# Locality-hashed attention with a gated projection: a planner that reckons with one queue of transfers, sigmoids by table, and a small load on another queue

## The chip, the cores and the metric

The kernel runs on one core of one Trainium2 chip. The metric is device time in microseconds of one execution. The core's engines run side by side, each through its own instructions in their order: TensorE (PE) multiplies matrices, VectorE (DVE) and ScalarE (ACT) work element by element and read its results, GpSimd (POOL) works element by element in on-chip memory, and SyncE (SP) issues transfers. Semaphores let an instruction of one engine wait for another engine or for a transfer.

## The reference

Attention over 4 batches, 8 heads, 768 rows and 64 columns per head, where a row sees only the rows with the same six hash bits; then a gated projection of the 3072 x 512 result, with 1536 hidden columns. Cut to what matters:

```python
q_bits = (np.einsum('bhsd,dk->bhsk', q, proj) > 0)           # six bits -> bucket; the same for k
mask = q_bucket[:, :, :, None] == k_bucket[:, :, None, :]
scores = np.where(mask, scale * np.matmul(q, k.transpose(0, 1, 3, 2)), -1e9)
attn = np.exp(scores - np.max(scores, axis=-1, keepdims=True))
attn = attn / (np.sum(attn, axis=-1, keepdims=True) + 1e-09)
x = np.matmul(attn, v)                                        # -> (3072, 512)
gate = 1.0 / (1.0 + np.exp(-(x @ w_gate)))
out = gate * (x @ w_val) @ w_out
```

The weights arrive as 64-bit floats and are turned into 32-bit ones on the chip.

## The kernel before, in words

**Stages.** The attention takes two heads at a time: 16 pairs, each in two groups of three 128-row tiles, 32 groups in all. For a pair, q and k are loaded (`load`, L968 and L977), turned on TensorE (`turn`, L1034), rounded to high and low parts (`high` L1054, `low` L1057), hashed (`hash_`, L1069; for the first pair `hash_first`, L1015) and the bits made (`bits`, L1076) and spread by small transfers (L1080, L1087). For a group come scores (L1162 for the bits, L1168 for the products), the row minimum that also evacuates them (`maximum`, VectorE, L1178), the exponential (`exponent`, ScalarE, L1186), turning of the exponentials (`turned`, L1219), a copy out of the banks (`whole`, L1226, on ScalarE or VectorE), the product with v (`values`, L1236), a reciprocal of the sums (`inverse`, L1193 on) that goes through memory (`told` L1200, `spread` L1207), the division on GpSimd (`divided`, L1246) and a store (L1249).

**The gated projection** has 12 blocks of hidden columns. Two of them (`J1 = 2`) are worked off during the attention, one unit for each batch and half of its rows, eight units: `moe_early` makes two gate products and two value products (`product`, L531), passes the gates through a sigmoid, multiplies (`gated`, L547 to L552), and makes an output product (L568). The other blocks follow after the attention, in `moe_pair` (L758, L877), fully on TensorE. Meanwhile the weights are converted (`converted`, L348 to L382) and split into parts (`split`, L405 to L415), which are stored and fetched again.

**The sigmoid in `moe_early`.** The batches 0 to 2 (six units) share the time with the attention. There ScalarE makes `exp(-z)` (L590), and VectorE adds one, bounds it and takes the reciprocal (`inverted`, L559 and L560). Batch 3 comes after the last attention group and uses ScalarE's sigmoid directly (`direct`).

**The order.** Each piece of work is a `Task` with a priority, an engine (or a choice of engines), a duration in ns, the tasks it waits for, and tokens for buffers that it takes and gives. `Plan.order` plays all tasks through with these durations, once, when the kernel is built: at each moment every free engine takes the ready task with the lowest key whose tokens are there. The sequence that comes out is the order in which each engine's instructions are written. On the chip nothing is reordered: a task that comes later than planned holds up what stands behind it on its engine. TensorE's tasks are also charged for a change of its tile division (`LEAVE`, `BEGIN`), and it may wait a while for another task of the same division (`PATIENCE`).

A transfer is a task of `sp`: 600 ns of issue, and a `tail` until it has landed, 2000 ns plus a ns for 200 bytes, whatever else is under way; where transfers crowd, a larger number of bytes is written instead (`CROWDED`). At most eight are reckoned to be under way (`landings`).

**The start.** The hash projection, 64 x 6 numbers, is loaded twice into a tile of weights by ScalarE's queue (`load_projection`, L277) behind the first q; `hash_weights` (L282 to L288, VectorE) then lays out the weights of the first hash. GpSimd clears tiles first (up to L294).

Of the kernel before, what the change touches and what calls it, by code (L numbers as in the profile page):

```python
# [24 lines left out]
HUGE = 2.0**126  # L25
# [4 lines left out]
SEEN = {"pe": 260, "act": 140, "pool": 130, "dve": 130, "sp": 0}  # L30
# [11 lines left out]
IN_FLIGHT = 8  # L42


class Task:
# [7 lines left out]
    def __init__(self, key, options, after, take, give, tail, kind, begun):  # L53
        self.key, self.options, self.take, self.give, self.tail = key, options, take, give, tail
# [12 lines left out]
class Plan:  # L67
# [5 lines left out]
    def __init__(self, stock):  # L73
        self.stock, self.tasks = dict(stock), []
        self.landings = [0] * IN_FLIGHT

    def add(self, key, engine, ns=None, emit=None, after=(), take=(), give=(), tail=0, kind="all", begun=()):
        options = engine if isinstance(engine, list) else [(engine, ns, emit)]
        t = Task((key, len(self.tasks)), options, after, take, give, tail, kind, begun)
        self.tasks.append(t)  # L80
        return t

    def order(self):
# [24 lines left out]
        while events:  # L108
# [10 lines left out]
            while again:  # L119
                again = False  # L120
                for e in SEEN:
# [58 lines left out]
def lsh_attention_glu_kernel(ctx, tc, q, k, v, proj, w_gate, w_val, w_out, out):  # L180
    nc = tc.nc
# [92 lines left out]
    def load_projection():  # L274
        for half in range(2):
            at_ = half * HS + NB
            nc.scalar.dma_start(hw["w"][half * D : (half + 1) * D, at_ : at_ + NB], proj)  # L277
# [57 lines left out]
    def converted(key, n, j, late, which, after, first):  # L335
# [48 lines left out]
        a = dma(key, CROWDED if late else 524288, load, after=after + last_load[late], take=[raw_])  # L384
# [4 lines left out]
        c1 = add(key, "dve", 440, mantissa, after=[b1], **both)  # L389
        c2 = add(key, "dve", 700, whole, after=[c1], **both)  # L390
        d = add(key, "dve", 700, signed, after=[b2, c2], take=["port"], give=[raw_, "port"])
        return z, add(key, "pool", 1300, lambda: scaled(nc.gpsimd), after=[d], **both)

    def split(key, src, to, size, late, after, give, tile_of=None):
# [16 lines left out]
        h = add(key, "act", 60 + 500 * part_, high, after=after, take=[wk] if tile_of is None else [])  # L411
        low_ = add(key, "pool", 100 + 1200 * part_, low, after=[h], take=["port"], give=give + ["port"])
        if tile_of is not None:
            return low_, low_
        return low_, dma(key, CROWDED if late else 1024 * size, lambda: nc.sync.dma_start(to, f(z["w"])), after=[low_], give=[wk])  # L415
# [19 lines left out]
    def combined(key, n, js, late, after):  # L435
# [26 lines left out]
        on = lambda fn: [("pool", 750, lambda: fn(nc.gpsimd)), ("dve", 350, lambda: fn(nc.vector))]  # L462
# [24 lines left out]
    def load_x(u, b, g, stored, ending):  # L487
# [19 lines left out]
        a = add(FIRST, "sp", 1200, load, after=stored + in_turn["x"], take=["xr"], tail=2000 + 786432 // 200)  # L507
# [50 lines left out]
    def inverted(j):  # L558
        nc.vector.tensor_scalar(sig[:, j], sig[:, j], 1.0, HUGE, op0=ALU.add, op1=ALU.min)  # L559
        nc.vector.reciprocal(sig[:, j], sig[:, j])  # L560

# [12 lines left out]
    def moe_early(key, b, g, stored, pace):  # L574
# [9 lines left out]
        for j in range(J1):  # L584
# [3 lines left out]
                FIRST, "act", 490,  # L588
                lambda j=j, z=z, fn=AF.Sigmoid if direct else AF.Exp, by=1.0 if direct else -1.0:
                    nc.scalar.activation(sig[:, j], z["acc"][:, :GN], fn, scale=by),  # L590
# [5 lines left out]
        else:  # L596
            s_ = [add(FIRST, "dve", 800, lambda j=j: inverted(j), after=[zs[j]], take=["port"], give=["port"]) for j in range(J1)]
# [40 lines left out]
    def x_pair(u, b, last_use):  # L638
# [35 lines left out]
        on = lambda fn: [("dve", 960, lambda: fn(nc.vector))]  # L674
        z["ready"], got = {}, {}

        def raw(name):
            got[name] = dma(
                FIRST + 0.5, 1200000 if u == "0_0" else 393216, lambda: load(name), after=stored[b, int(name[1]) - 1] + [later["switch"]], take=[f"r{name}"],
# [8 lines left out]
        def pieces_of(name):  # L688
            h = add(FIRST, "act", 850, lambda: high(name), after=[got[name]], take=[f"x{name}"])
# [28 lines left out]
    def fetch_piece(at_, js, slot, n, m, after, first):  # L718

        def go():  # L720
# [11 lines left out]
            1e3, CROWDED if first else CROWDED // 4, go,  # L732
# [8 lines left out]
    def group(key, at_, n, js, slot, x, sig_, final, free_w, hslot, prev):  # L741
# [34 lines left out]
        def snap(m, name):  # L776
            told[name] = add(
                FIRST, "act", 480, lambda: nc.scalar.copy(tile_(name, "sn"), bank[m]), after=[done[m]], take=["sn"], give=["z"],  # L778
            )

        def plus(m, y, name, after=(), give=("z",), tag=None):
            def go():
# [3 lines left out]
                FIRST, "dve", 560, go, after=[done[m], told[y]] + list(after), take=[tag] if tag else [], give=list(give),  # L786
            )

        def finish(where):
            a = told[where]  # L790
            if n == "g":
                sig_[where] = z, add(
                    FIRST, "act", 490, lambda: nc.scalar.activation(z[where], z[where], AF.Sigmoid), after=[a]
# [20 lines left out]
            c = add(FIRST, "act", 510, hi, after=[b], take=[f"h{hslot}{jj}{uu}"])  # L814
# [34 lines left out]
    def moe_pair(key, i, b, prev):  # L849
# [45 lines left out]
        def ended(t, prev, first, last):  # L895
# [15 lines left out]
            if first:  # L911
# [4 lines left out]
                FIRST, "dve", 690, lambda: nc.vector.tensor_add(obs[t], accs[t], obs[t]), after=[prev, ended_[t]],  # L916
# [37 lines left out]
    def pair(i):  # L954
# [134 lines left out]
        if i == 0:  # L1089
            pass  # L1090
        here = {
            n: add(t0 - 10.72, "act" if i == 0 and n == "q" else "sp", 1200 if n == "q" else 2400,
                   lambda n=n: load(n, nc.scalar if i == 0 and n == "q" else nc.sync), tail=4000, take=[n + "r"],
# [3 lines left out]
        if i == 0:  # L1097
            first_loads.extend(here.values())
            hw["loaded"] = add(t0 - 10.5, "act", 1200, load_projection, after=[])
            hw["landed"] = add(0, "pool", 0, lambda: None, after=[hw["loaded"], add(0, "pool", 4500, lambda: None)])  # L1100
# [25 lines left out]
        else:  # L1126
            a = add(t0 - 2.6, "pe", 4 * MM, hash_, after=plains + [hw["task"]], take=["two"], kind="hash")
            bits_ = add(t0 - 2.6, "dve", 480, bits, after=[a], give=["two"])
            needs.append(add(t0 - 2.6, "sp", 1200, spread_q, after=[bits_], tail=2500))
            needs.append(add(t0 - 2.6, "sp", 2400, lambda: spread_k(nc.sync), after=[bits_], tail=2500))  # L1130
        for m, n in enumerate("qk"):
            n_ = t0 - 3.4 + m * 0.5
            b_ = add(n_, [("act", 690, lambda n=n: high(n, nc.scalar.copy)), ("dve", 870, lambda n=n: high(n, nc.vector.tensor_copy))],
                     after=[plains["kq".index(n)]])
            ways = [("dve", 960, lambda n=n: low(n, nc.vector)), ("pool", 2000, lambda n=n: low(n, nc.gpsimd))]
# [5 lines left out]
            if n == "q" and i:  # L1141
                needs += [add(n_, "sp", 1200, lambda x=x: swapped(x), after=[y], tail=4000) for x, y in (("h", b_), ("l", c_))]
        if i == 0:
            first_loads.extend(needs)
        v_here = dma(t0 - 5, 393216, load_v, take=["vr"], after=first_loads[:2] + [last_loads.get("v")])
# [5 lines left out]
    def attend(i, g, z, needs, v_here):  # L1151
# [100 lines left out]
        for t in range(GT):  # L1252
# [16 lines left out]
        a = add(n, "dve", 560, inverse, after=exps, take=["sv"], give=["su"])  # L1269
        a = add(n, "sp", 600, told, after=[a], tail=2500, give=["sv"])  # L1270
# [122 lines left out]
```

## Time and profile before

| | |
|---|---|
| median of 3 runs | 1007.04 us (1006.73 to 1011.49) |
| the profiled execution | 1011.25 us, of which the span of the instructions is 1009.5 us |
| TensorE busy | 976.2 us (97%) |
| VectorE busy | 793.6 us (79%) |
| ScalarE busy | 544.8 us (54%) |
| GpSimd busy | 270.4 us (27%) |
| mean granted TensorE clock | 0.991 |
| first scores (L1162) | 18.78 us after the first instruction |

The numbers come from one profiled execution. A busy share is a mean over stages with different limits. Matrix products are pipelined, so a busy TensorE need not be at its peak, and a lowered clock shows as busy time. The "chain that ended last" is followed back from the last instruction, at each step to what released it or to the instruction ahead of it on its engine; "issue" in it is time in which the engine waited for nothing that the profile shows.

### The profile page before, as it was taken

To read this page: it belongs to the slowest core of one execution; us is meant where nothing else is said; L and a number is where in the kernel's file an instruction comes from. 1 tells how busy PE (TensorE), PEld (TensorE's weight loads), DVE (VectorE), ACT (ScalarE), POOL (GpSimd) and SP (SyncE) were. 2 spreads that over 40 slices of the span, in tenths; PEclk is the share of its full clock that TensorE was granted. 3 is DMA by queue.
4 is the path that set the end of the run, shared out by engine and by line. 5 is a ranking of instruction groups with operands and counts; after the bars stand their busy time and mean duration, and the time that the engine had idled before them with its cause. 6 is when DMAs were issued, how large, how long until landed. Compare 5 with 4: busy or idle time off the path is not lost.

```text
span 1009.5 us, 20877 instructions
## 1 busy us (share of the span) xinstructions
PE 976.2 (97%) x8091; PEld 781.9 (77%) x8092; DVE 793.6 (79%) x1467; ACT 544.8 (54%) x1016; POOL 270.4 (27%) x243
## 2 busy tenths in 40 slices
PE   7999997999999989899999999999999999999998
PEld 4666565666666666666679999999989989999897
DVE  6888997788798877788848877788777778787864
ACT  3878874777867857677634442353333425242330
POOL 1234463635555546355430121211100000000000
PEclk9999998999999999999999999999999999999999
DMA  5555584656676557455469977569469680505121
GB/s 132 130 161 166 136 226 143 191 171 192 204 221 179 186 166 221 150 163 184 143 221 397 370 242 283 203 239 357 153 201 368 212 281 10 188 17 172 35 91 62
DMA packets 144346, 190.95 MB, mean 189 GB/s; under 512 B 64728, under 2 KB 103032, under 8 KB 144248
## 3 DMA queue, kind: packets, MB, share of 16 engines
q1 hardware_dynamic: 142520, 189.24, 57.9%
q8 instruction: 63, 1.03, 0.4%
q10 hardware_dynamic: 1728, 0.40, 0.2%
q14 instruction: 35, 0.29, 0.1%
HBM read 127.41 MB, written 49.28 MB: 175 GB/s over the span
## 4 chain that ended last, share of the span: by engine, by line
PE 80%; DVE 12%; DMA 2%; ACT 2%; issue 2%; SPq 1%; POOL 0%; DVEq 0%; POOLq 0%; ACTq 0%
PE yo L877 16%; PE pv L1236 10%; PE sc L1168 6%; PE tp L1219 5%; DVE e L1178 5%; PE zo L568 4%; PE sc L1162 3%; PE zv L531 2%; PE zg L531 2%; PE z1g L758 2%; PE z4v L758 2%; PE z1v L758 2%; PE z6g L758 2%; PE z5g L758 2%; PE z2g L758 2%
## 5 line engine op out<-in xcount | busy, mean ns | idle before, releaser
L1186 ACT ACTIVATE e<-e,st 128x768 f32<-128x768 f32 x192 | 179.0, 933 | 64.2 <-DVE e L1178 64.1
L1178 DVE TENSOR_SCALAR_CACHE_REDUCE e<-sc 128x768 f32<-128x768 f32 x192 | 176.3, 950 | 33.9 <-PE sc L1168 33.2
L1236 PE MATMUL pv<-ef,vr 128*64 128x384 f32 x768 | 140.6, 499 | 2.6 <-ACT ef L1226 2.5
L1219 PEld LDWEIGHTS tp<-ident,e 64*128 64x128 f32 x2304 | 86.1, 139 | 47.3 <-issue 16.4
L1219 PE MATMUL tp<-ident,e 64*128 64x64 f32 x2304 | 98.5, 227 | 11.1 <-DVE e L1178 6.8
L1226 ACT COPY ef<-tp 128x768 f32<-128x768 f32 x107 | 84.0, 795 | 22.0 <-PE tp L1219 21.4
L1226 DVE COPY ef<-tp 128x768 f32<-128x768 f32 x85 | 80.7, 952 | 17.4 <-PE tp L1219 17.0
L1236 PEld LDWEIGHTS pv<-ef,vr 128*64 128x64 f32 x768 | 49.0, 137 | 57.0 <-issue 46.2
L1168 PE MATMUL sc<-kh,ql 64*128 64x384 f32 x192 | 90.5, 472 | 0.0
L1168 PE MATMUL sc<-kh,qsl 64*128 64x384 f32 x192 | 90.5, 471 | 0.0
L1162 PE MATMUL sc<-kb,qb 64*128 64x384 bf16 x384 | 65.6, 332 | 7.9 <-DVE e L1178 4.4
L1168 PE MATMUL sc<-kh,qh 64*128 64x384 f32 x192 | 64.7, 337 | 0.0
L1168 PE MATMUL sc<-kh,qsh 64*128 64x384 f32 x192 | 64.7, 337 | 0.0
L1168 PE MATMUL sc<-kl,qsh 64*128 64x384 f32 x192 | 64.4, 336 | 0.0
L1168 PE MATMUL sc<-kl,qh 64*128 64x384 f32 x192 | 64.4, 335 | 0.0
L1162 PEld LDWEIGHTS <-qb 64*128 64x128 bf16 x384 | 22.2, 94 | 51.7 <-issue 43.0
L778 ACT COPY snm1g<-z1g 128x384 f32<-128x384 f32 x20 | 9.6, 479 | 79.8 <-PE z1g L758 79.7
L916 DVE TENSOR_TENSOR ol<-yo,ol 128x512 f32<-128x512 f32 x36 | 24.8, 688 | 29.4 <-PE yo L877 29.4
L382 POOL TENSOR_TENSOR exg<-mfg,exg 128x512 f32<-128x512 f32 x12 | 15.7, 1305 | 109.5 <-DVE exg L377 109.5
L877 PE MATMUL yo<-wo,gh 128*128 128x512 f32 x144 | 44.5, 390 | 0.0
L1057 POOL TENSOR_TENSOR kl<-kx,kh 128x768 fp32r<-128x768 f32 x16 | 29.9, 1870 | 38.7 <-DVE kh L1054 26.2
L1246 POOL TENSOR_TENSOR xs<-xs,rb 128x384 f32<-128x384 f32 x32 | 33.2, 1039 | 24.7 <-DVE xs L1243 15.7
(590 smaller groups left out, 2851.8 us busy)
## 6 DMA issues: line engine op xcount, KB each, us to landing
wg<-kg SPq DMA_DIRECT2D x33, 512.0 KB
wv<-kv SPq DMA_DIRECT2D x33, 512.0 KB
ra<-xd SPq DMA_DIRECT2D x32, 384.0 KB
wo<-ko SPq DMA_DIRECT2D x22, 512.0 KB
part<-ob SPq DMA_DIRECT2D x36, 256.0 KB
kg<-pkg SPq DMA_DIRECT2D x15, 512.0 KB
kv<-pkv SPq DMA_DIRECT2D x15, 512.0 KB
kr<-in_k_dram SPq DMA_DIRECT2D x64, 96.0 KB
```

The lines of the kernel that those rows point to most:

```text
L531: nc.tensor.matmul(z["acc"][:, :GN], a[:, wc], x[xx][c // 2][:, c % 2, :], start=(c == 0 and i == 0), stop=(c == KC - 1 and i == 2),)
L568: nc.tensor.matmul(acc, a[:, slot, ts_], w, start=(first and i == 0), stop=(last and i == 2))
L758: nc.tensor.matmul(bank[m], a[:, wc], x[xx, block][:, c, :], start=(c == 0 and i == 0), stop=(c == 1 and i == 2),)
L877: nc.tensor.matmul(accs[t], a[:, ts_], w, start=(start and jj == 0 and q == 0), stop=(stop and jj == 1 and q == 2),)
L1162: nc.tensor.matmul(sc[:, j, :GN], z["qb"][rows, beyond if j else c], z["kb"][rows, h], start=True, stop=False, tile_position=(j * D, 0),)
L1168: nc.tensor.matmul(sc[:, j, :GN], q_[rows, c], z["k" + x][rows, h * GN : (h + 1) * GN], start=False, stop=(m == 2), tile_position=(j * D, 0),)
L1178: nc.vector.tensor_scalar(sp(e), gz["sc", t, h][:, :, :GN], MASKED, None, op0=ALU.min, op1=ALU.min, accum_out=gz["st", t][:, h : h + 1],)
L1186: nc.scalar.activation(e, e, AF.Exp, bias=st[:, h : h + 1], scale=-1.0, accum_out=gz["su"][:, h * GT + t : h * GT + t + 1],)
L1219: nc.tensor.transpose(tp[:, r, at_ : at_ + D], gz["e", t, h][rows, c * P : (c + 1) * P], ident[rows, rows], tile_position=(r * D, 0),)
L1226: copy(gz["ef", c].rearrange("p (n r d) -> p r n d", r=2, d=D), gz["tp", c][:, :, :GN].rearrange("p r (n d) -> p r n d", d=D),)
L1236: nc.tensor.matmul(gz["pv"][rows, :GN], z["v"][:, h, c], gz["ef", c][:, h * GN : (h + 1) * GN], start=(c == 0), stop=(c == NC - 1), tile_p ...
L1246: nc.gpsimd.tensor_mul(gz["xs"], gz["xs"], gz["rb"])
```

## The change

- Sigmoid: for batches 0 to 2, ScalarE copies both gate products out of their banks, then runs one sigmoid over both at once (768 columns). `inverted` and its two VectorE instructions go.
- Transfers in the plan: a transfer moves its data in one queue shared by all (`moving`), for a time given with the task, mostly bytes / 355 ns; it begins at the earliest 900 ns after the issue begins and is seen 1000 ns after its data. `CROWDED` goes.
- Periods in the plan: nearly all durations on VectorE, ScalarE, GpSimd and SP are set anew.
- The projection: `load_projection` issues from GpSimd's queue and is a task of `pool`. The time at which its landing is reckoned moves from a task of `pool` (4500 ns) to an engine of the plan only (`timer`, 4000 ns).

```diff
+BEFORE, BEHIND_IT = 900, 1000
...
-                    if e == "sp" and t.tail:
-                        free[e] = max(now, self.landings[0]) + ns
-                        self.landings = self.landings[1:] + [free[e] + t.tail]
+                    landed = 0
+                    if t.dmas:
+                        n_, moved = t.dmas
+                        if e == "sp":
+                            free[e] = max(now, self.landings[0]) + ns
+                        self.moving = max(self.moving, free[e] - ns + BEFORE) + moved
+                        landed = max(self.moving, free[e] + BEFORE // 2) + BEHIND_IT - free[e]
+                        if e == "sp":
+                            self.landings = (self.landings + [free[e] + landed] * n_)[n_:]
                     at(free[e], "free", e)
-                    seen = free[e] + t.tail + SEEN[e]
+                    seen = free[e] + (landed or SEEN[e])
...
-            nc.scalar.dma_start(hw["w"][half * D : (half + 1) * D, at_ : at_ + NB], proj)
+            nc.gpsimd.dma_start(hw["w"][half * D : (half + 1) * D, at_ : at_ + NB], proj)
...
-    CROWDED = 1600000
-
     def dma(key, nbytes, emit, **kw):
-        return add(key, "sp", 600, emit, tail=2000 + nbytes // 200, **kw)
+        return add(key, "sp", 550, emit, dmas=(1, nbytes / 355), **kw)
...
-        b1 = add(key, "dve", 440, exponent, after=[a], take=[token] * first + ["port"], give=["port"])
-        b2 = add(key, "act", 700, shifted, after=[b1])
+        b1 = add(key, "dve", 345, exponent, after=[a], take=[token] * first + ["port"], give=["port"])
+        b2 = add(key, "act", 620, shifted, after=[b1])
...
-    def inverted(j):
-        nc.vector.tensor_scalar(sig[:, j], sig[:, j], 1.0, HUGE, op0=ALU.add, op1=ALU.min)
-        nc.vector.reciprocal(sig[:, j], sig[:, j])
...
-                FIRST, "act", 490,
-                lambda j=j, z=z, fn=AF.Sigmoid if direct else AF.Exp, by=1.0 if direct else -1.0:
-                    nc.scalar.activation(sig[:, j], z["acc"][:, :GN], fn, scale=by),
+                FIRST, "act", 490 if direct else 375,
+                lambda j=j, z=z, fn=AF.Sigmoid if direct else AF.Copy: nc.scalar.activation(sig[:, j], z["acc"][:, :GN], fn),
...
-            s_ = [add(FIRST, "dve", 800, lambda j=j: inverted(j), after=[zs[j]], take=["port"], give=["port"]) for j in range(J1)]
+            s_ = [add(FIRST, "act", 3400, lambda: nc.scalar.activation(sig, sig, AF.Sigmoid), after=zs)] * J1
...
-        a = add(FIRST, "sp", 1200, load, after=stored + in_turn["x"], take=["xr"], tail=2000 + 786432 // 200)
+        a = add(FIRST, "sp", 1050, load, after=stored + in_turn["x"], take=["xr"], dmas=(2, 2600))
...
-            hw["loaded"] = add(t0 - 10.5, "act", 1200, load_projection, after=[])
-            hw["landed"] = add(0, "pool", 0, lambda: None, after=[hw["loaded"], add(0, "pool", 4500, lambda: None)])
+            hw["loaded"] = add(t0 - 10.5, "pool", 1200, load_projection)
+            hw["landed"] = add(0, "timer", 0, lambda: None, after=[hw["loaded"], add(0, "timer", 4000, lambda: None)])
...
-            b_ = add(n_, [("act", 690, lambda n=n: high(n, nc.scalar.copy)), ("dve", 870, lambda n=n: high(n, nc.vector.tensor_copy))],
+            b_ = add(n_, [("act", 735, lambda n=n: high(n, nc.scalar.copy)), ("dve", 480, lambda n=n: high(n, nc.vector.tensor_copy))],
...
-                    n + 1.25, "act", 1025, lambda t=t, h=h: exponent(t, h), after=[least[h]] + exps[-1:],
+                    n + 1.25, "act", 928, lambda t=t, h=h: exponent(t, h), after=[least[h]] + exps[-1:],
...
-        a = add(n, "sp", 600, told, after=[a], tail=2500, give=["sv"])
-        spread_ = add(n, "sp", 1200, spread, after=[a], tail=3500, take=["rb"])
+        a = add(n, "sp", 680, told, after=[a], dmas=(1, 80), give=["sv"])
+        spread_ = add(n, "sp", 1250, spread, after=[a], dmas=(2, 680), take=["rb"])
```

More of the change, by code (lines that the diff above doesn't have):

```diff
@@ L74, in __init__, with add @@
         self.stock, self.tasks = dict(stock), []
-        self.landings = [0] * IN_FLIGHT
-    def add(self, key, engine, ns=None, emit=None, after=(), take=(), give=(), tail=0, kind="all", begun=()):
+        self.landings, self.moving = [0] * IN_FLIGHT, 0
+    def add(self, key, engine, ns=None, emit=None, after=(), take=(), give=(), dmas=None, kind="all", begun=()):
         options = engine if isinstance(engine, list) else [(engine, ns, emit)]
-        t = Task((key, len(self.tasks)), options, after, take, give, tail, kind, begun)
+        t = Task((key, len(self.tasks)), options, after, take, give, dmas, kind, begun)
         self.tasks.append(t)
@@ L382, in scaled @@
             eng.tensor_mul(f(z["ex"]), f(z["mf"]), f(z["ex"]))
-        a = dma(key, CROWDED if late else 524288, load, after=after + last_load[late], take=[raw_])
+        a = dma(key, 600000, load, after=after + last_load[late], take=[raw_])
         last_load[late] = [a]
         both = dict(take=["port"], give=["port"])
-        b1 = add(key, "dve", 440, exponent, after=[a], take=[token] * first + ["port"], give=["port"])
-        b2 = add(key, "act", 700, shifted, after=[b1])
[L389 to L392, printed above, removed]
+        b1 = add(key, "dve", 345, exponent, after=[a], take=[token] * first + ["port"], give=["port"])
+        b2 = add(key, "act", 620, shifted, after=[b1])
+        c1 = add(key, "dve", 345, mantissa, after=[b1], **both)
+        c2 = add(key, "dve", 605, whole, after=[c1], **both)
+        d = add(key, "dve", 605, signed, after=[b2, c2], take=["port"], give=[raw_, "port"])
+        return z, add(key, "pool", 1250, lambda: scaled(nc.gpsimd), after=[d], **both)
     def split(key, src, to, size, late, after, give, tile_of=None):
@@ L678, in raw @@
             got[name] = dma(
-                FIRST + 0.5, 1200000 if u == "0_0" else 393216, lambda: load(name), after=stored[b, int(name[1]) - 1] + [later["switch"]], take=[f"r{name}"],
+                FIRST + 0.5, 440000, lambda: load(name), after=stored[b, int(name[1]) - 1] + [later["switch"]], take=[f"r{name}"],
             )
@@ L731, in fetch_piece @@
         made[at_, js, n, m] = last_fetch[role] = dma(
-            1e3, CROWDED if first else CROWDED // 4, go,
+            1e3, 1024 * (HF if m == 3 and n != "o" else DM), go,
             after=[made_piece[key_], later["switch" if slot else "first"], last_fetch.get(role)] + after, take=[role],
@@ L777, in snap @@
             told[name] = add(
-                FIRST, "act", 480, lambda: nc.scalar.copy(tile_(name, "sn"), bank[m]), after=[done[m]], take=["sn"], give=["z"],
+                FIRST, "act", 385, lambda: nc.scalar.copy(tile_(name, "sn"), bank[m]), after=[done[m]], take=["sn"], give=["z"],
             )
@@ L785, in plus @@
             told[name] = add(
-                FIRST, "dve", 560, go, after=[done[m], told[y]] + list(after), take=[tag] if tag else [], give=list(give),
+                FIRST, "dve", 476, go, after=[done[m], told[y]] + list(after), take=[tag] if tag else [], give=list(give),
             )
@@ L792, in finish @@
                 sig_[where] = z, add(
-                    FIRST, "act", 490, lambda: nc.scalar.activation(z[where], z[where], AF.Sigmoid), after=[a]
+                    FIRST, "act", 430, lambda: nc.scalar.activation(z[where], z[where], AF.Sigmoid), after=[a]
                 )
@@ L813, in finish @@
             low_ = lambda eng: eng.tensor_sub(z["h", where][1], z[where], f(z["h", where][0]))
-            c = add(FIRST, "act", 510, hi, after=[b], take=[f"h{hslot}{jj}{uu}"])
+            c = add(FIRST, "act", 425, hi, after=[b], take=[f"h{hslot}{jj}{uu}"])
             sig_["h", where] = add(
@@ L1288, in attend @@
         a = add(n - 6, either(summed), after=[prev], take=["xs"], give=["one"] + ["moe"] * ends)
-        a = add(n - 4, "pool", 1050, divided, after=[a, spread_], take=["port"], give=["rb", "port"])
+        a = add(n - 4, "pool", 965, divided, after=[a, spread_], take=["port"], give=["rb", "port"])
         stored[b, g].append(dma(n, 196608, store, after=[a], give=["xs"]))
```

39 lines of the change are left out of this document (19 added, 20 removed).

## The prediction

> **What bounds the kernel now.** I read the page's busy shares and chain first, then stretches of the span cut where TensorE stops, then the chain in order of time, then the start. The page:
>
> ```profile
> PE 976.2 (97%) x8091; PEld 781.9 (77%) x8092; DVE 793.6 (79%) x1467; ACT 544.8 (54%) x1016; POOL 270.4 (27%) x243
> PE 80%; DVE 12%; DMA 2%; ACT 2%; issue 2%; SPq 1%; POOL 0%; DVEq 0%; POOLq 0%; ACTq 0%
> ```
>
> TensorE is the bound, but 12% of the chain that ended last, 121 us, is VectorE. The stretches tell where; columns are the stretch, its length, each engine's busy time, granted clock, DMA share, GB/s:
>
> ```profile
> 0.00:18.78 18.78, 13.54 (x75) 6.66 (x77) 10.20 (x40) 5.47 (x7) 4.51 (x13) 0.91 0.75 168
> 18.78:160.00 141.22, 131.86 (x1664) 86.28 (x1665) 118.20 (x238) 112.12 (x208) 59.56 (x47) 1.00 0.61 164
> 160.00:180.00 20.00, 17.08 (x141) 12.71 (x138) 16.05 (x26) 8.82 (x17) 7.67 (x8) 0.83 0.36 118
> 180.00:285.00 105.00, 104.61 (x1210) 71.26 (x1211) 88.58 (x171) 80.86 (x153) 55.06 (x47) 1.00 0.64 194
> 285.00:292.00 7.00, 5.86 (x76) 4.59 (x74) 6.94 (x9) 3.76 (x9) 1.27 (x1) 1.00 0.47 134
> 292.00:360.00 68.00, 67.07 (x759) 45.88 (x756) 54.02 (x104) 50.84 (x97) 40.46 (x37) 1.00 0.63 191
> 360.00:378.00 18.00, 14.53 (x154) 10.10 (x154) 15.88 (x26) 10.68 (x20) 5.52 (x5) 0.91 0.45 142
> 416.00:430.00 14.00, 11.31 (x120) 9.79 (x120) 11.15 (x21) 9.34 (x19) 4.09 (x3) 0.88 0.18 66
> 430.00:495.00 65.00, 64.25 (x754) 41.77 (x750) 55.84 (x114) 49.62 (x95) 35.11 (x33) 1.00 0.56 177
> 495.00:520.00 25.00, 22.45 (x218) 15.14 (x217) 16.34 (x24) 13.91 (x25) 10.30 (x9) 1.00 0.38 131
> 544.00:1009.50 465.50, 461.62 (x2421) 430.01 (x2419) 355.13 (x623) 163.60 (x309) 25.83 (x24) 1.00 0.56 198
> ```
>
> From 544 us on TensorE is busy but for the last 3.9 us; nothing the change touches can shorten that. Before, the loss sits in five short stretches. Idle time plus time lost to a lowered clock (length times one minus the clock): 160 to 180: 2.9 + 3.4 = 6.3; 285 to 292: 1.1; 360 to 378: 3.5 + 1.6 = 5.1; 416 to 430: 2.7 + 1.7 = 4.4; 495 to 520: 2.6. Together **19.5 us**. The rest of the attention stage is idle for 9.4 us up to 160 and 0.4 + 0.9 + 0.8 after it, **11.5 us**. Now the chain in order of time (start, length, what):
>
> ```profile
> 161.88 2.55 DVE sig L560
> 165.30 1.85 issue
> 221.84 2.55 DVE sig L560
> 286.62 2.55 DVE sig L560
> 362.00 2.55 DVE sig L560
> 365.82 2.33 issue
> 406.64 2.44 issue
> 495.93 2.55 DVE sig L560
> 508.08 2.43 issue
> ```
>
> Each of the five stretches has a reciprocal of the gate (L560) in it or ahead of it. The four "issue" pieces are reciprocals too: each lies behind one and lasts about as long. So nine of the twelve stand on the path, and five of these groups leave TensorE without work. The prices behind it:
>
> ```profile
> L559 DVE TENSOR_SCALAR sig<-sig x12: 296/355/1156, 161.5 to 507.7; 128x384 f32<-128x384 f32 x12
> L560 DVE RECIPROCAL sig<-sig x12: 2552/2553/2554, 161.9 to 508.0; 128x384 f32<-128x384 f32 x12
> L590 ACT ACTIVATE sig<-zg x16: 468/490/493, 142.7 to 540.3; 128x384 f32<-128x384 f32 x16
> L590 ACT ACT_TABLE_LOAD  x1: 1283/1283/1283, 519.7 to 519.7; - x1
> L778 ACT COPY snm1g<-z1g 128x384 f32<-128x384 f32 x20 | 9.6, 479 | 79.8 <-PE z1g L758 79.7
> L1226 ACT COPY ef<-tp 128x768 f32<-128x768 f32 x107 | 84.0, 795 | 22.0 <-PE tp L1219 21.4
> ```
>
> The old plan charged 800 ns for a task (tensor_scalar, reciprocal) that lasts 355 + 2553 = 2908 ns. Two per unit put VectorE 4.2 us behind its plan, and everything behind them in its queue was late: the maxima (L1178) that free score banks and release ScalarE's exponentials.
>
> **The change, part by part.**
>
> *Sigmoid.* VectorE loses 12 x 2.908 = 34.9 us of its 793.6. ScalarE gets, per unit, one sigmoid over 768 elements and two table loads, since exponentials stand on both sides. The sigmoid is the 384-element one plus what 384 more cost in a copy: 490 + (795 - 479) = 806 ns. A unit is 806 + 2 x 1283 = 3.37 us, six units 20.2 us; the last may need no load back. The new plan charges 3.4 us, so it knows the block. The twelve exponentials become copies: 12 x (490 - 479) = 0.1 us. What hides the block: in the five stretches ScalarE is idle for 11.2, 3.2, 7.3, 4.7 and 11.1 us. What now waits: exponentials queued behind it, and both gate products (L547), which wait for both gates where the first could go after its own; the value products (L531) lie between and cover that. What the block still costs TensorE no row shows. From below it is 0, for it fits the idle time just counted; from above it is 5.1 us per unit, the stretch 360 to 378 over again. I take 1.1 us, the smallest stall of the five, as the block is no longer than that idle time in four of the five and in the plan: 6 x 1.1 = 6.6. So this part: -19.5 + 6.6 = **-12.9 us**.
>
> *The projection through GpSimd's queue.* The start:
>
> ```profile
> 0.73 1.28 ACT L235 ACT_TABLE_LOAD   x1 [0.73 <-PEq L1377]
> 2.02 0.20 ACT L235 ACTIVATE warm<-warm 128x1 f32<-128x1 f32 x1
> 2.93 4.18 ACTq L277 DMA_DIRECT2D hw<-in_proj_dram  x2
> 3.06 0.24 POOL L294 MEMSET su<- 128x32 f32 x3
> 6.99 0.17 DVE L282 TENSOR_SCALAR hw<-hw 64x6 f32<-64x6 f32 x1 [2.37 <-DMA hw<-in_proj_dram]
> 9.10 1.80 POOL L1057 TENSOR_TENSOR kl<-kx,kh 128x768 fp32r<-128x768 f32 x1 [5.79 <-ACT kh L1054]
> 9.44 1.49 DVE L282 TENSOR_SCALAR hw<-hw 64x6 f32<-64x6 f32 x1 [2.29 <-DMA hw<-in_proj_dram]
> 11.57 2.90 PE L1015 MATMUL hk<-kx,w 128*128 128x384 f32 x4 [3.45 <-DVE w L288]
> 14.26 1.56 PE L1015 MATMUL hq<-qx,w 128*128 128x384 f32 x4
> 18.78 0.34 PE L1162 MATMUL sc<-kb,qb 64*128 64x384 bf16 x2
> ```
>
> Two issues leave ScalarE's queue, which has nothing due until the first transposes come, and go to GpSimd's, behind its memsets (end 3.30) and ahead of its first subtraction at 9.10, which sat idle 5.79 us before. No engine's work moves; what can move is the second landing at 9.42, on which the hash weights wait. On ScalarE's queue the two were issued over 4.18 us, behind two loads of q. On GpSimd's own queue there is nothing ahead. If they take no longer than the first did (issued 2.93, seen at 6.99, 4.06 us), the second lands near 3.3 + 0.6 + 4.06 = 8.0: 1.4 us earlier. Then VectorE's second step also comes before GpSimd's subtraction, beside which it took 1.49 us against 0.17 alone (1.3 us), and the first hash, which stood idle 3.45 us before and ran in a start with a mean clock of 0.91, may take the second's 1.56 instead of 2.90 us (1.3 us). Upper bound: 4.0 us. Lower bound: an issue on GpSimd that takes the whole 4.18 us again lands at 3.3 + 4.18 + 2.9 = 10.4, a loss of 1.0. I take **-3.0 us**, nearer the end where the two follow-on gains come with an arrival before 9.1. On this the Trainium skill ("SBUF — State Buffer", section "SBUF: two separate sides") speaks against the change: a DMA issued from GpSimd has its descriptors written by GpSimd, which a VectorE operation in a two-port mode locks out meanwhile. No run here shows it; by it the term would be 0 and the sum -10.9 us.
>
> *One queue of transfers, measured periods.* No instruction's work changes, only who comes when in each queue. Two transfers of the chain:
>
> ```profile
> 153.38 3.92 DMA kg<-pkg
> 411.46 3.08 DMA rd<-sv
> ```
>
> A 512 KB store took 3.92 us from issue on; the old plan said 0.6 + 2.0 + 2.6 = 5.2, the new one 0.9 + 1.5 + 1.0 = 3.4 with nothing ahead of it and more with a backlog. The small store of the sums took 3.08; the old plan said 0.6 + 2.5 = 3.1, the new one says 0.7 + 0.45 + 1.0 = 2.1 at least, so here it reckons too early; its reader is GpSimd's division, off TensorE's path. The engines' periods come down to the rows: 1025 to 928 for an exponential (933 on the page), 700 to 605, 870 to 480 for a cast. What a new order is worth no row gives: at best the 11.5 us of idle time that I have not tied to the gates, at worst two new stalls like the first stretch, 12.6 us. I take +2: the transfers' reckoning is nearer for the large ones, too early for the small.
>
> **Sum:** -12.9 - 3.0 + 2 = -13.9 us. The profiled execution took 1011.25 us (span 1009.5), which gives 997.3; it stands 4.2 us over the median of 1007.04, and from that the forecast is 1007.0 - 13.9 = **993**.
>
> **Rivals.**
> *The block on ScalarE takes most of it back.* For: exponentials must wait 3.4 us at a time. Against: ScalarE's idle time above. At 2.6 us each the six cost 15.6, and the start brings 2: 1007 - 19.5 + 15.6 - 2 = 1001, and with the order's +2 about 1003.
> *ScalarE becomes the late engine (slower).* If exponentials come late by so much that TensorE stops and its clock falls each time, each of the six units costs the 5.1 us of 360 to 378: 30.6, less 19.5 and less 3, plus the order's 2: 1017. It decides once the block outlasts ScalarE's idle time in a stretch, as in 285 to 292, where it has 3.2 us for 3.4.
> *Loads cost more than their row.* If ScalarE also stood still after each load by as much again as the load, a unit would be 3.37 + 2 x 1.28 = 5.9 us, 15 us more in all, and with all of it on the path the time 993 + 15 = 1008. Against: the first load ends at 2.01 and the next activation starts at 2.02. Such a rule stands in the Trainium skill ("ScalarE: Activation LUTs", section "What ACT_TABLE_LOAD costs"): 1283 ns and some 1380 ns of drain. The 1283 agrees with this trace, the drain after the load it does not show.
> *More than I count.* The new order also takes the 11.5 us and the block costs nothing: 1007 - 19.5 - 11.5 - 3 = 973; half of the former, 979.
> *The projection is not earlier:* 996; inside the forecast's range.
>
> **How the numbers follow.** About 0.5%, 5 us, is what a measurement of this kernel can tell (its three runs span 4.8). Forecast 0.60 (own range 985 to 1001), more than I count 0.08: faster 0.68. The block takes it back 0.14, loads dearer 0.04: within 0.5% 0.18. Slower 0.14. The range reaches from 980, half of the "more" case, to 1010, which leaves out the slower case and a few in 100 below.
>
> **What would show it.** Right: no L560; six sigmoids and eleven or twelve loads of 1283 ns on ScalarE; VectorE's busy time near 759 us; clock 1.00 between 160 and 430; first scores (L1162) near 15 to 16 us instead of 18.78; TensorE's idle time before 544 down by about 10 us and the late stage, now 465.5, the same length. Wrong: TensorE waiting behind ScalarE's exponentials after each sigmoid, stalls in the stretch before 160, where no gate runs, or a gap where the late stage's first weights land.

## The result, and the profile after

The changed kernel takes 998.06 us (median of 6 runs, 995.0 to 1001.59), the kernel before 1008.21 us (6 runs); the ratio is 0.9893 [0.9862, 0.9924], which is a gain of 10.8 us. Forecast were 993 in a range of 980 to 1010, and a gain of 13.9. The profiled execution of after took 997.94 us (span 996.2), close to its median; that of before, 1011.25, stands 3.0 us above its own, so what a profile of before says is up to 3 us too long.

The page of after, the same two lines as were shown of before (busy time of each engine, and its share of the chain that ended last):

```profile
PE 969.6 (97%) x8092; PEld 777.3 (78%) x8092; DVE 775.6 (78%) x1460; ACT 554.0 (56%) x1015; POOL 271.9 (27%) x245
PE 83%; DVE 7%; DMA 4%; ACT 3%; SPq 2%; issue 1%; POOL 1%; DVEq 0%; ACTq 0%; POOLq 0%
```

VectorE's share of the chain falls from 12% to 7%. The stretches of after, again cut where TensorE stops:

```profile
18.21:130.00 111.79, 104.16 (x1325) 66.34 (x1326) 93.09 (x193) 88.35 (x162) 39.96 (x29) 1.00 0.54 143
130.00:160.00 30.00, 28.34 (x334) 20.77 (x332) 24.35 (x47) 23.96 (x46) 19.18 (x18) 1.00 0.72 216
160.00:325.00 165.00, 163.90 (x1856) 111.94 (x1853) 140.19 (x274) 129.94 (x238) 100.44 (x89) 1.00 0.71 212
325.00:352.00 27.00, 24.25 (x271) 16.69 (x273) 21.66 (x41) 19.25 (x33) 13.86 (x13) 1.00 0.70 225
400.00:416.00 16.00, 12.87 (x123) 10.21 (x120) 9.41 (x21) 11.78 (x19) 6.40 (x7) 0.89 0.87 268
530.00:996.20 466.20, 462.17 (x2423) 430.35 (x2421) 354.85 (x617) 161.59 (x305) 24.70 (x23) 1.00 0.56 194
```

From 160 to 325 us TensorE is idle for 1.1 us; before, its two stalls there cost 7.4. The five stretches that held 19.5 us have gone; in their place stand two smaller stalls, 2.75 us (325 to 352) and 3.13 + 1.76 us of lowered clock (400 to 416). Up to 160 us nothing is won: 7.6 + 1.7 us of idle time, 9.4 before. The last stage keeps its length. The new gates, as groups of a line (durations min/median/max, first and last start):

```profile
L596 ACT ACT_TABLE_LOAD  x6: 1283/1283/1283, 156.9 to 493.2; - x6
L596 ACT ACTIVATE sig<-sig x6: 843/847/848, 158.2 to 494.5; 128x768 f32<-128x768 f32 x6
L1185 ACT ACT_TABLE_LOAD  x5: 1283/1283/1283, 161.5 to 408.5; - x5
```

Eleven loads, and 847 ns for the sigmoid (806 estimated). ScalarE's order around one of them:

```profile
332.68 0.47 ACT L589 ACTIVATE sig<-zg 128x384 f32<-128x384 f32 x1
333.17 1.28 ACT L596 ACT_TABLE_LOAD   x1
334.47 0.85 ACT L596 ACTIVATE sig<-sig 128x768 f32<-128x768 f32 x1
335.22 0.39 ACT L409 CAST pkv<-exv 128x256 fp32r<-128x256 f32 x1
335.52 0.62 ACT L409 CAST pkv<-t12v 128x512 fp32r<-128x512 f32 x1
336.16 1.28 ACT L1185 ACT_TABLE_LOAD   x1
337.45 0.94 ACT L1185 ACTIVATE e<-e,st 128x768 f32<-128x768 f32 x1
```

Each load is followed at once by its activation. ScalarE's wait for the store of a weight part, 4.12 us ahead of the first reciprocal before (157.38, shown under e1), is 0.43 us here:

```profile
154.97 0.62 ACT L409 CAST pkg<-t34g 128x512 fp32r<-128x512 f32 x1 [0.43 <-DMA kg<-pkg]
```

What is new is VectorE waiting for raw weight blocks (`exponent`, L364 after, L360 before). First what its engine waited for, of after (us, times), then of before, then the largest wait, of after:

```profile
  DMA rawv<-in_moe_w_val_dram: 8.5, 5
  DMA rawg<-in_moe_w_gate_dram: 3.4, 3
```

```profile
  DMA rawo<-in_moe_w_out_dram: 0.9, 1
  DMA rawg<-in_moe_w_gate_dram: 0.4, 1
```

```profile
407.29 0.43 DVE L364 TENSOR_SCALAR exv<-rawv 128x512 int32<-128x512 int32 x1 [5.36 <-DMA rawv<-in_moe_w_val_dram]
```

11.9 us instead of 1.3. Both new stalls lie behind such a block; the chain of after, in order of time, has them. In the first of the two it also runs through the sigmoid (334.47) and the load behind it (336.16) shown above, so that stall is not the raw block's alone.

```profile
323.39 5.38 DMA rawv<-in_moe_w_val_dram
402.10 5.17 DMA rawv<-in_moe_w_val_dram
```

The new plan reckons 600000 / 355 ns of transfer for such a block, so 0.9 + 1.7 + 1.0 = 3.6 us where nothing is ahead of it; the old one said 5.2 us in this stage.

### The profile page after: what moved, and what is told of

Read it like the earlier page. It is cut to its first block, busy times and chain, and to the rows that moved or that the text cites. A ratio compares the mean times of both kernels' runs of the same rounds, so it can differ in the third digit from the quotient of the medians.

```text
span 996.2 us, 20856 instructions
## 1 busy us (share of the span) xinstructions
PE 969.6 (97%) x8092; PEld 777.3 (78%) x8092; DVE 775.6 (78%) x1460; ACT 554.0 (56%) x1015; POOL 271.9 (27%) x245
## 4 chain that ended last, share of the span: by engine, by line
PE 83%; DVE 7%; DMA 4%; ACT 3%; SPq 2%; issue 1%; POOL 1%; DVEq 0%; ACTq 0%; POOLq 0%
PE yo L876 17%; PE pv L1235 10%; PE sc L1167 7%; PE tp L1218 6%; PE zv L535 3%; PE zo L568 3%; PE sc L1161 3%; PE zg L535 3%; DVE e L1177 3%; PE z1g L757 2%; PE z7g L757 2%; PE z4v L757 2%; PE z1v L757 2%; PE z5g L757 2%; PE z4g L757 2%; PE z3g L757 2%
## 5 line engine op out<-in xcount | busy, mean ns | idle before, releaser
L1218 PEld LDWEIGHTS tp<-ident,e 64*128 64x128 f32 x2304 | 83.8, 138 | 42.2 <-issue 16.6
L1225 DVE COPY ef<-tp 128x768 f32<-128x768 f32 x93 | 87.7, 951 | 20.2 <-PE tp L1218 20.0
L1218 PE MATMUL tp<-ident,e 64*128 64x64 f32 x2304 | 96.3, 226 | 7.0 <-DVE e L1177 3.4
L1225 ACT COPY ef<-tp 128x768 f32<-128x768 f32 x99 | 77.7, 794 | 27.3 <-PE tp L1218 26.9
L1161 PE MATMUL sc<-kb,qb 64*128 64x384 bf16 x384 | 65.0, 331 | 9.5 <-DVE e L1177 5.8
L1161 PEld LDWEIGHTS <-qb 64*128 64x128 bf16 x384 | 22.2, 94 | 49.3 <-issue 41.1
L535 PE MATMUL zg<-xh,wg 128*128 128x384 f32 x128 | 37.5, 348 | 0.1
```

What stands on the lines that cost most here:

```text
L535: nc.tensor.matmul(z["acc"][:, :GN], a[:, wc], x[xx][c // 2][:, c % 2, :], start=(c == 0 and i == 0), stop=(c == KC - 1 and i == 2),)
L1161: nc.tensor.matmul(sc[:, j, :GN], z["qb"][rows, beyond if j else c], z["kb"][rows, h], start=True, stop=False, tile_position=(j * D, 0),)
L1218: nc.tensor.transpose(tp[:, r, at_ : at_ + D], gz["e", t, h][rows, c * P : (c + 1) * P], ident[rows, rows], tile_position=(r * D, 0),)
L1225: copy(gz["ef", c].rearrange("p (n r d) -> p r n d", r=2, d=D), gz["tp", c][:, :, :GN].rearrange("p r (n d) -> p r n d", d=D),)
```

## The experiments

The numbered runs were timed in five rounds against the kernel before. "First scores" is the start of the first L1162 (L1161 after) of the profiled execution, "attention" the time from there to its last product with v, "rest" from there to the last matrix product.

| run | median us | ratio to before | profiled us | first scores | attention | rest |
|---|---|---|---|---|---|---|
| before | | 1 | 1011.25 | 18.78 | 495.8 | 491.0 |
| after | 998.06 | 0.9893 [0.9862, 0.9924] | 997.94 | 18.21 | 484.2 | 489.8 |
| e1_sig_only | 999.64 | 0.9923 [0.9900, 0.9945] | 1000.74 | 19.60 | 484.0 | 491.5 |
| e2_no_sigmoid | 1009.21 | 1.0010 [0.9992, 1.0028] | 1007.39 | 19.02 | 492.0 | 490.6 |
| e3_honest_charge | 1013.51 | 1.0061 [1.0037, 1.0084] | 1010.91 | 17.93 | 487.7 | 499.7 |
| e4_projection_back | 999.85 | 0.9919 [0.9894, 0.9944] | 1003.82 | 19.13 | 488.9 | 490.1 |
| e5_sp_periods | 1001.62 | 0.9917 [0.9896, 0.9938] | 999.99 | 18.83 | 481.1 | 494.4 |
| e6_raw_later | 996.53 | 0.9868 [0.9842, 0.9893] | 995.04 | 16.38 | 483.0 | 489.7 |
| e7_more_loads | 1001.55 | 0.9915 [0.9895, 0.9936] | 1000.33 | 18.27 | 486.5 | 489.8 |
| e8_start | 998.36 | 0.9883 [0.9860, 0.9906] | 997.51 | 16.19 | 485.6 | 490.0 |
| e9_kl_vector | 996.93 | 0.9886 [0.9867, 0.9906] | 996.08 | 15.18 | 485.5 | 489.7 |
| e10_kl_vector_act_queue | 995.15 | 0.9877 [0.9854, 0.9900] | 993.84 | 15.61 | 482.5 | 490.0 |
| e11_old_periods | 1004.10 | 0.9963 [0.9946, 0.9981] | 1004.10 | 19.68 | 489.2 | 489.4 |
| e12_raw_later_kl | 993.45 | 0.9856 [0.9837, 0.9876] | 993.07 | 15.27 | 481.6 | 490.1 |

e1 to e4 ran on one chip, e5 to e8 on a second, e9 to e12 on a third; medians are compared within such a group, else ratios.

**e1_sig_only**: the kernel before with the sigmoid's part alone.

```diff
...
-            s_ = [add(FIRST, "dve", 800, lambda j=j: inverted(j), after=[zs[j]], take=["port"], give=["port"]) for j in range(J1)]
+            s_ = [add(FIRST, "act", 3400, lambda: nc.scalar.activation(sig, sig, AF.Sigmoid), after=zs)] * J1
```

> The kernel before with the sigmoid by its table alone (copies charged 375, the sigmoid 3400); transfers, periods and the projection's queue as before. Theory A (the reciprocals' 34.9 us leave VectorE): most of the 10.2 us measured for the whole change is here, so 996 to 1000 us, no stretch of half clock at a gate. Theory C (the new reckoning of transfers and periods gives the gain): 1004 to 1008.

Measured: -7.8 us (0.9923). From 175 us to the end of the attention TensorE is idle for 2.7 us in all, so four of the forecast's five stretches go with the reciprocals alone. The first is still there although no reciprocal is. Stretches of e1, and ScalarE's longest wait of the first:

```profile
152.00:175.00 23.00, 17.64 (x178) 12.23 (x175) 15.11 (x29) 13.77 (x23) 8.45 (x7) 0.85 0.70 196
175.00:503.60 328.60, 325.89 (x3695) 224.09 (x3694) 260.06 (x510) 253.07 (x461) 173.12 (x155) 1.00 0.63 191
```

```profile
160.87 0.62 ACT L405 CAST pkg<-t34g 128x512 fp32r<-128x512 f32 x1 [6.72 <-DMA kg<-pkg]
```

ScalarE waits 6.72 us for the store of a weight part to free its buffer, and the exponentials stand behind it; between the two, on the chain, stands the sigmoid with its two loads (161.90 to 165.30). Before has the same wait at the same place, ahead of its first reciprocal at 161.9:

```profile
157.38 0.62 ACT L405 CAST pkg<-t34g 128x512 fp32r<-128x512 f32 x1 [4.12 <-DMA kg<-pkg]
```

The store was issued late by SP, 153.38 us before and 156.71 in e1, behind issues that take longer than the plan says. The timeline of SP in before:

```profile
137.47 1.63 SPq L1080 DMA_DIRECT2D qb<-qb  x2
139.15 4.62 SPq L1087 DMA_DIRECT2D kb<-qb  x4
```

The plan said 1.2 and 2.4 us, and e1 has 1.62 and 3.00; e5, below, tests whether that is the cause. The same stretch of e2, the next run, has the reciprocals (153.10 and 162.03, both on its chain) beside the changed kernel's times for SP:

```profile
150.00:180.00 30.00, 27.04 (x287) 19.01 (x283) 26.06 (x46) 19.45 (x38) 14.14 (x12) 1.00 0.68 203
```

It loses 3.0 us, at full clock. So the first and largest stall was not the reciprocals' alone: where it is largest, a late store stands ahead of the gates, of either kind. How its 6.3 us divide between the two isn't shown.

**e2_no_sigmoid**: the changed kernel with the two exponentials and `inverted` back, charged as before.

> The changed kernel with the old sigmoid (exponential, tensor_scalar, reciprocal; charged 490 and 800 as before), all else changed. Theory A: the reciprocals stall the cores as before, 1004 to 1010 us, with half clock behind a reciprocal. Theory C: most of the gain stays, 997 to 1001.

Measured: +1.0 us (1.0010). Projection, transfers and periods without the sigmoid gain nothing; with it the changed kernel is 11.8 us faster than e2. The sigmoid is worth 7.8 us on the old plan and 11.8 on the new one; the intervals of the four ratios don't tell these two apart. In e2 the plan still reckons the reciprocals at 800 ns. No run reckons them rightly in the new plan, so how much of the 11.8 comes from VectorE being freed and how much from a block that the plan knows stays open.

**e3_honest_charge**: the kernel before, `inverted` charged 2910 ns instead of 800; the reciprocals stay.

> The kernel before with one number changed: the task of tensor_scalar and reciprocal is charged 2910 ns instead of 800. Theory A (the work itself): VectorE still has 34.9 us of it, so at most a third of the gain, 1003 to 1008 us. Theory B (only the plan's error hurts): the stalls go without taking any work off VectorE, 996 to 1001.

Measured: +6.1 us (1.0061), slower than either forecast. The stretches of the attention and of the hand-over to the last stage, of e3, and then the same of before:

```profile
17.93:505.60 487.67, 471.59 (x5469) 317.85 (x5468) 393.87 (x756) 371.15 (x688) 229.22 (x199) 0.99 0.59 171
505.60:525.00 19.40, 11.14 (x42) 8.56 (x43) 10.13 (x15) 7.09 (x12) 9.30 (x8) 0.74 0.58 206
```

```profile
18.78:514.60 495.82, 473.01 (x5457) 320.20 (x5456) 410.27 (x777) 363.04 (x678) 235.79 (x202) 0.99 0.58 173
514.60:525.00 10.40, 9.02 (x43) 7.59 (x44) 4.99 (x8) 4.24 (x8) 4.23 (x4) 1.00 0.62 192
```

Reckoning the reciprocals rightly takes 8.1 us from the attention, where removing them took 11.6 to 11.8. It loses 8.7 in the rest, most of it at the hand-over, where TensorE is idle for 8.3 us at a clock of 0.74: the pieces of the chain there are GpSimd's conversion and split of weights, ahead of the last x that the next products (L531) need:

```profile
509.62 3.34 issue
513.00 1.27 POOL exo L382
514.99 1.27 POOL pko L408
517.37 1.33 ACT xh L501 x3
518.76 1.64 DVE xl L505
520.45 4.74 PE zg L531 x20
```

Part of what the attention saves is work put off: blocks of `w_out` are converted (`exo`) by 59 instructions of VectorE, ScalarE and GpSimd inside the attention before, and by 48 in e3, whose other 12 come behind it. So an honest number alone is no gain for the kernel, and how much of the loss inside the attention was the plan's error isn't shown.

**e4_projection_back**: the changed kernel with the projection issued from ScalarE's queue again, as a task of ScalarE.

> The changed kernel with the projection issued from ScalarE's queue again (charged 1200 to it). The prediction gave the move 3.0 us; the trace of the changed kernel shows the first scores only 0.57 us earlier. If the move is worth 3: 1001 us and first scores near 21. If it is worth what the trace shows: within 1 us of 998, first scores at 18.2 to 19.

Measured: 0.9919, 2.6 us behind the changed kernel with intervals that overlap. Scores start at 19.13 us instead of 18.21. On VectorE, ScalarE, GpSimd and SP the order is that of the changed kernel but for the two issues, so the run compares the queues; but its profiled execution is the slowest of its six (995.88 to 1003.82), and the attention of 488.9 us against 484.2 is no measure of the queue. e9 and e10 repeat the comparison.

**e5_sp_periods**: e1 with only the issue times of SP from the change (q's bits 1720, k's 3040, loads of q and k 1300 and 2100, and the small ones); tails as before.

> The sigmoid by its table on the kernel before (as in the first experiment, 7.8 us faster than before), and only SP's issue periods taken from the change; landings still by the old tails. In the first experiment TensorE stands 5.4 us at 161 us and then runs at half clock for 6.8 us, behind a store of weight parts that SP issues late. If SP's periods are what the plan had wrong there, that stall (8.8 us) goes: 990 to 994. If it is the old landing times, it stays: 998 to 1001.

Measured: 0.9917. Its stretches, the old stall and the hand-over:

```profile
152.00:175.00 23.00, 23.00 (x244) 16.16 (x242) 18.29 (x35) 18.76 (x34) 14.52 (x15) 1.00 0.62 188
495.00:530.00 35.00, 30.50 (x154) 25.47 (x151) 15.95 (x26) 11.00 (x21) 1.98 (x2) 0.90 0.83 306
```

With SP's issues reckoned at what they take, the stall of e1 is gone (23.00 busy of 23.00, clock 1.00), though the time is not under 994 as was expected then. Its attention is 2.9 us shorter than that of e1, but the total doesn't move, because the rest is 2.9 us longer: the hand-over loses 4.5 us of idle time and 35 x 0.10 = 3.5 of clock. The chain there has the load of x behind weight fetches.

```profile
501.25 9.18 DMA wo<-ko
510.50 7.24 DMA xr<-xd
```

**e6_raw_later**: the changed kernel; the landing of a raw block is reckoned 1.8 us later, its time in the queue is unchanged.

```diff
...
-        a = dma(key, 600000, load, after=after + last_load[late], take=[raw_])
+        a = dma(key, 600000, load, more=1800, after=after + last_load[late], take=[raw_])
```

> The changed kernel with the landing of a raw weight block reckoned 1.8 us later, its time in the queue of transfers unchanged. VectorE waits 11.9 us for raw blocks in the changed kernel and 1.3 us in the kernel before; at 400 to 416 us one such wait costs TensorE 3.1 us and 1.7 us of clock, at 325 to 352 another 2.8 us. If the new reckoning of these landings is the new wait: VectorE's waits for raw blocks under 4 us and 991 to 995 us. If other work takes the place: within 2 us of the changed kernel's 998.

Measured: 0.9868, 996.53 against 998.36 of e8, which has the changed kernel's order. The waits of VectorE for raw blocks, of e6:

```profile
  POOL pko L412: 5.3, 4
  DMA rawg<-in_moe_w_gate_dram: 2.6, 1
```

One wait of 2.6 us for a block instead of eight of 11.9; in part it is now a buffer that is late, freed by GpSimd's split (5.3). The clock is 1.00 all through its attention, which lasts 483.0 us instead of 484.2. The gain in time is 1.8 us, less than one run can tell; e12 against e9, below, gives 3.5 for the same edit (1.7 against e10).

**e7_more_loads**: the changed kernel with two more table loads and two one-column activations behind each sigmoid, charged 6400 ns.

```diff
...
+                nc.scalar.activation(warm, warm, AF.Exp)
+                nc.scalar.activation(warm, warm, AF.Sigmoid)
```

> The changed kernel with two more table loads and two one-column activations behind each of the six sigmoids, 3.0 us more on ScalarE per unit, the task charged 6400. If ScalarE has room, as its idle time in these stretches says: within 2 us of 998. If the block lies on the path: up to 6 x 3.0 = 18 us more, 1005 to 1016.

Measured: 1001.55, 3.2 us over e8 (by the ratios, 2.2 over the changed kernel). ScalarE's busy time is 573.1 us, 19.1 more. So a second block of nearly that length, known to the plan, costs about 0.5 us a unit (3.2 / 6); the intervals of e7, e8 and the changed kernel overlap. That the first block is as cheap is argued from this, not measured.

**e8_start**: the changed kernel, in whose plan the first `kl` (the low part of the first pair's k, a subtraction on GpSimd) waits for the hash weights.

> The changed kernel with the first pair's subtraction on GpSimd (kl) made to wait for the hash weights; one copy of these took VectorE 1.69 us beside it and 0.16 without. First scores at about 16 us instead of 18.2. If an earlier start is kept to the end: 995.5 to 997; if the attention takes it back: 998.

Measured: 0.9883. Every engine's order came out as in the changed kernel, so this is that kernel once more: its scores begin at 16.19 us in one profiled execution and at 18.21 in another. That shows how far the start varies, and not what a start is worth, as each median has starts of its own. In both, one of four small VectorE copies fell beside GpSimd's subtraction of `kl`; in e8, whose loads landed 0.24 us earlier, it was the last:

```profile
8.94 1.81 POOL L1056 TENSOR_TENSOR kl<-kx,kh 128x768 fp32r<-128x768 f32 x1 [4.48 <-ACT kh L1053]
8.99 1.79 DVE L294 COPY w<-hw 64x24 f32<-64x24 f32 x1
```

**e9_kl_vector**: the changed kernel, the first pair's `kl` on VectorE. **e10_kl_vector_act_queue**: the same with the projection on ScalarE's queue.

> The changed kernel with the first pair's low part of k (kl) subtracted on VectorE instead of GpSimd; every other instruction in the same order. Two runs of the changed kernel's order showed first scores at 18.2 and at 16.2 us, by whether one or several steps of the hash weights fall beside kl on GpSimd (1.7 to 1.8 us for one step). Without kl there the steps take 0.17 us each: first scores at 15.5 to 16.5 us, clock not lowered in the start. If the attention keeps an earlier start: 1 to 2 us under the changed kernel (0.987 of before); if not, 0.988 to 0.989.

> The same with the projection on ScalarE's queue; the engines' order is the same but for that issue. It measures the queue by itself. If the queue is worth what the prediction counted for the landing alone (1.4 us): first scores 1 to 2 us later than in its neighbour and the time 0 to 2 us longer. If the gain of the start was the collision with kl and not the queue: first scores within 0.5 us of its neighbour.

Measured: 0.9886 and 0.9877. The second landing as VectorE sees it, of e9 and then of e10 (first scores at 15.18 and 15.61):

```profile
8.82 0.17 DVE L288 TENSOR_SCALAR hw<-hw 64x6 f32<-64x6 f32 x1 [0.40 <-DMA hw<-in_proj_dram]
```

```profile
9.25 0.17 DVE L288 TENSOR_SCALAR hw<-hw 64x6 f32<-64x6 f32 x1 [2.41 <-DMA hw<-in_proj_dram]
```

Without the collision the scores start 3.0 us earlier than in the changed kernel's profile and 1.0 earlier than in that of e8; the ratios (0.9886, 0.9877 against 0.9893) are lower by less than their intervals. The queue alone is 0.43 us at the start, and no gain in the time (996.93 on GpSimd's queue, 995.15 on ScalarE's, their runs overlapping).

**e11_old_periods**: the changed kernel with the old periods of VectorE, ScalarE and GpSimd; the sigmoid, the new transfers and SP's periods stay.

> The changed kernel with the old periods of VectorE, ScalarE and GpSimd in the plan (25 numbers), the sigmoid and all of SP's reckoning kept. If the measured periods carry a part of the gain: 1000 to 1004. If the sigmoid and the transfers carry it: 996 to 999. If the periods cost something: under 996.

Measured: 0.9963, 7.1 us slower than the changed kernel and 4.0 slower than e1, which has the old periods, the old transfers and the projection on its old queue. TensorE is idle for 13.6 us before 170 us, where the changed kernel has 9.3 up to the same time:

```profile
19.68:170.00 150.32, 136.76 (x1708) 90.22 (x1708) 119.71 (x240) 120.21 (x218) 62.20 (x49) 0.99 0.56 153
```

So the new transfers and SP's new times, with the projection moved, are a loss with the old periods (e11 against e1), and with the new ones a gain of 3.0 over e1, with intervals that overlap: the parts don't add.

**e12_raw_later_kl**: e6 and e9 together.

> The changed kernel with the raw blocks reckoned 1.8 us later and kl on VectorE: the two edits together. If both gains add: 993 to 996, 0.984 to 0.986 of before. If the second is taken back in the attention: 0.986 to 0.988.

Measured: 993.45 us (993.01 to 995.71), 0.9856 [0.9837, 0.9876], the lowest median of all; e9 on the same chip took 996.93 (994.8 to 999.8), and the interval of the changed kernel just overlaps. Its attention runs at full clock:

```profile
15.27:496.90 481.63, 466.97 (x5462) 314.51 (x5461) 382.95 (x761) 377.73 (x688) 237.87 (x204) 1.00 0.65 189
```

## Why the prediction was right, and where it was not

*The sum, -13.9 against -10.8.* The sigmoid carries the gain, as was forecast. That the sum came so near is in part luck: the projection's 3.0 isn't shown to have come, and the order, counted as a loss of 2, may be a gain.

*The sigmoid, -12.9.* Right as the main term and in its mechanism: -11.8 from e2 to the changed kernel, though -7.8 alone (e1). Two of its sizes were wrong, in opposite directions. The gain of 19.5 counted all of the 6.3 us of 160 to 180 as the reciprocals' because one stood in the chain there; the failed step is "each of the five stretches has a reciprocal in it or ahead of it". The wait of 4.12 us for a store, ahead of the reciprocal, was in the trace of before (157.38), and e1 keeps the stall. In the changed kernel the wait is 0.43 us and the stall gone; e5 shows that SP's issue times alone can remove it. The charge of 6.6 for ScalarE's blocks was probably too dear: e7 adds a second such block per unit for 0.5 us each. With none of the 6.3, so 13.2 of gain, and about 3 of charge the term would have been -10.

*The projection, -3.0.* The size was wrong, and in the time not even the direction is shown: scores 0.57 us earlier in the profile, and of the two comparisons of the queues one favours GpSimd's (e4, by 2.6 us), the other ScalarE's (e10, by 0.9), both inside their intervals. The landing came at 8.65 instead of the 8.0 worked out, as a load took 4.7 to 4.8 us from its issue instead of 4.06; then one step still fell beside `kl`, for 1.69 us; and the first hash, which was to save 1.3 us, took 2.19 + 2.52 us instead of 2.90 + 1.56. In e9, without the collision, it took 1.53 + 1.45. The premise that an earlier start is an earlier end is neither shown nor refuted (below). On the rule of the Trainium skill quoted in the prediction ("SBUF — State Buffer", section "SBUF: two separate sides"): the trace can't tell whether VectorE held up GpSimd's issue; it was at work until 4.62 us, while the two were issued (3.26 to 4.46), and idle for the 3.44 us ahead of the first landing. The same section's other rule, that the shared port is held for a whole instruction, agrees with the copy of 1.79 us beside `kl` in e8, which ends at 10.78 us, 0.03 behind `kl`; alone it takes 0.17.

*Order, transfers and periods, +2.* By order of adding, the rest of the change (with the projection) is worth +1.0 without the sigmoid and -3.0 on top of it, neither clear of the intervals, so the forecast's -1 for the two terms lies between. The failed step is that the transfers' reckoning is nearer for the large ones: that holds for the store (3.92 us, 3.4 reckoned now and 5.2 before), but the raw loads that matter take 5.2 to 5.4 against 3.6 reckoned now with nothing ahead of them and 5.2 before, and they became the new waits.

*Rivals.* The block taking its gain back and ScalarE as the late engine asked for 15.6 and 30.6 us of six blocks; six more of nearly the same length cost 2 to 3 (e7). Dearer loads fall by the trace and by e7, where 12 more of them with 12 small activations add 19.1 us to ScalarE's busy time. The drain that the Trainium skill gives ("ScalarE: Activation LUTs", section "What ACT_TABLE_LOAD costs") is seen on neither side of a load: the activation ahead ends at 333.15 and the load starts at 333.17; it ends at 333.17 + 1.28 = 334.45 and the activation starts at 334.47. The "more than I count" case (973, half of it 979) was not reached: e12, the best run, takes another 3.7 us by the ratios.

*What would show it.* VectorE's busy time fell to 775.6, not 759: nearly half of the difference is that the planner gave VectorE eight more copies of the turned exponentials, 93 instead of 85.

```profile
L1225 DVE COPY ef<-tp 128x768 f32<-128x768 f32 x93 | 87.7, 951 | 20.2 <-PE tp L1218 20.0
L1225 ACT COPY ef<-tp 128x768 f32<-128x768 f32 x99 | 77.7, 794 | 27.3 <-PE tp L1218 26.9
```

That left ScalarE with 99 copies instead of 107, 6.3 us less. The clock between 160 and 430 was not 1.00 throughout (0.89 from 400 to 416). TensorE's idle time in the attention fell by 5.7 us, not 10: 495.82 - 473.01 = 22.8 before, and after, by the stretch of its whole attention,

```profile
18.21:502.40 484.19, 467.09 (x5462) 315.77 (x5461) 388.63 (x770) 373.28 (x678) 237.00 (x204) 1.00 0.63 188
```

17.1. Another 4.9 came from the clock, whose loss in the stretches went from 6.7 to 1.8. The late stage kept its length.

What stays open is whether an earlier start is kept. Five runs have one order of instructions, but for the projection's queue and the engine of the first `kl` (after, e4, e8, e9, e10), and the attention of their profiled executions lasts 482.5 to 488.9 us. The 1.4 and 1.3 us that e8 and e9 seem to lose there (485.6 and 485.5 against 484.2) are well inside that spread; e10 starts 2.6 us earlier and its attention is 1.7 shorter. By the ratios e8, e9 and e10 lie 0.7 to 1.6 us under the changed kernel, less than their intervals.

## What to carry to other kernels

In an order written ahead of time, an instruction reckoned too short can do harm through what stands behind it, but correcting one number alone moved the loss elsewhere here (e3, e5); so look at the place where the stages meet after each correction. Before a stall is laid to the instruction in the chain, read what the other engines waited for just ahead of it. A switch of activation tables that the plan knows, on an engine with idle time, cost a fraction of its length here (e7). Before a stage of one profile is compared with that of another, see how far it varies between executions of nearly the same order: here by up to 6.4 us of the attention.

## What the hardware showed that was not expected

- A VectorE copy of 64 x 24 numbers took 1.69 to 1.79 us beside a GpSimd subtraction of 128 x 768, and 0.17 us alone.
- Two small loads of the projection, issued from GpSimd from 3.26 us on (the second, by the chain, at 3.94), were seen at 8.07 and 8.65: 4.8 and 4.7 us.
- Two of the raw weight blocks of 512 KB on the chain took 5.38 and 5.17 us; the stretches behind and around them (325 to 352, 400 to 416) moved 225 and 268 GB/s.
- The spread of k's bits, four issues on SP, took 2.99 to 3.14 us in ten of the first eleven times before, and 4.62 in the one at 139.15, ahead of the late store.
